# Spreading the preparation of a second layer's operands: sums of x one or two to a slot, earlier fetches, splits one to a position

## The chip, the cores and the metric

One core of one Trainium2 chip runs the whole program. The metric is the time of one execution on the device in microseconds. All times below are either whole executions, or come from one execution that the hardware profiler recorded.

## The reference, cut to what matters

A linear attention feeds two dense layers ("MoE" by name, with one expert), each a product, an activation and a product. The tokens number 2304, the model width is 512, the inner width 2048, everything is float32 (the weights come as 64-bit floats).

```python
x = attention(q, k, v)                 # 2304 x 512
h = x @ w_in1                          # 2304 x 2048
g = where(h >= 1, h, where(h <= -1, 0, (h + 1)**2 / 4))
x = g @ w_out1                         # 2304 x 512
h = x @ w_in2
g = h * tanh(log1p(exp(h)))            # Mish
out = g @ w_out2
```

## The kernel before, in words

**Precision.** A float32 operand is split into a high part (ScalarE writes a copy rounded to the fast matmul type, `high_part`, line 642) and a low part (what is left of it, a subtraction, `low_part`, line 645). Each product is then three matmuls: high by high, high by low, low by high (`three`, line 510). So each operand costs ScalarE (ACT) one pass and VectorE (DVE) or GpSimd (POOL) another before TensorE (PE) may read it.

**The first layer** goes over 6 blocks of 384 tokens (`n`) and over 16 chunks of the inner width (`c`). One step is a *slot*: `slot(i)` (line 969) does `gemm1` of chunk i (12 matmuls), its activation, and `gemm2` of the chunk three slots earlier (12 matmuls). The activation of slot i is on ACT and DVE in slot i; in slot i+1 ACT writes the high part of the result and POOL its low part (tile `ghl`, line 548). Slots 80 to 95 are the last block. What else has to be done in a slot stands in the table `ahead2`, by slot number, and is issued between `gemm1` and the activation.

**The second layer** multiplies 2 x 2 blocks of matrices with seven products in place of eight. The order of the seven is `ORDER = (1, 6, 7, 5, 4, 3, 2)`. The tokens form 3 groups (`g`) of two blocks, the inner width 8 units (`u`). `unit(g, u)` does seven products of 6 matmuls; the place of one in the row of all 168 is a *position*, 56 to a group, 7 to a unit. After each, DVE adds the PSUM result into the tiles `u`, `high`, `low`; after the last two ACT applies Mish to `high` and `low`, POOL forms four sums of them (`s`), and SyncE (SP) stores all to the DRAM buffer `gd`. What else is to be done stands in the table `places`, by position. Then `product` (line 790) multiplies by the last weights: 21 products of 72 matmuls, each in four parts (`pairs`); for these SP loads pieces from `gd` (tile `gq`, `g_load`, line 763), and ACT and DVE split them (tile `gc`, `g_split`, line 769).

**Operands of the second layer.** Four of the seven x operands of a group are differences and sums of blocks of x: `x_load` reads four blocks (tile `xq`), `x_sums` (line 686) forms them on POOL in four additions that depend on each other, `x_store` writes them to the DRAM buffer `xk`. Later `x_fetch` reads an operand back (tile `xf`), `x_high` and `x_low` split it (tile `xc`). The weights lie ready in the DRAM buffer `wk`; for a unit `w2_fetch` reads two pieces (384 KB and 512 KB), and `w2_high` and `w2_low` split them (tiles `w2p`, `w2q`). `w2_whole` and `x_operand` (lines 1010 and 1018) enter these steps in a table: the fetch at `at`, the high part at `at + apart`. In `ahead2` `apart` is 1 (slots), in `places` 8 or 6 (positions).

**What sets the order.** From slot 80 on all engines issue in the order in which the code is written: each engine has its own queue, and a step that waits holds up what stands behind it on that engine. All DMAs of this stretch are issued by SP's queue; eight semaphores, used in turn, mark their landing, so that a DMA is issued only when the eighth before it has landed. The tiles are taken in turn from two pools of buffers (`big`, 36, and `small`, 22), and a tile waits until the last reader of its buffer is done.

Of the kernel before, what the change touches and what calls it, by code (L numbers as in the profile page):

```python
# [64 lines left out]
def tile_attention_two_moes(  # L65
# [13 lines left out]
    nc = tc.nc  # L79
# [20 lines left out]
    table = const.tile([P, 1], F32, name="table")  # L100
# [145 lines left out]
    def add(eng, out, a, b, sub=True):  # L246
        eng.tensor_tensor(out=out, in0=a, in1=b, op=ALU.subtract if sub else ALU.add)  # L247
# [435 lines left out]
                t = xq[g, "q", r, c] = get([P, 2, TB], F32, "xq")  # L683
                nc.sync.dma_start(out=t, in_=yd[2 * g + c][:, 2 * r:2 * r + 2, :])

    def x_sums(g):
        b11, b12, b21, b22 = (xq[g, "q", r, c] for r in range(2) for c in range(2))
        add(nc.gpsimd, b11, b12, b11)
        add(nc.gpsimd, b12, b22, b12)
        add(nc.gpsimd, b22, b22, b11)  # L690
        add(nc.gpsimd, b21, b21, b22)

    def x_store(g):
        for i, at in enumerate(((0, 0), (1, 1), (0, 1), (1, 0))):
# [308 lines left out]
    ahead2, places, steps = {}, {}, {}  # L1003
    last = (NB - 1) * NF
    per_unit, per_group = len(ORDER), len(ORDER) * len(units)

    def put(table, key, job, *args):
        table.setdefault(key, []).append(partial(job, *args))

    def w2_whole(table, u, at, apart):  # L1010

        put(table, at, w2_fetch, 0, u, 0, 3)
        put(table, at, w2_fetch, 0, u, 3, 4)
        for x, which in enumerate((0, 2, 3, 1)):
            put(table, at + apart + x * apart // 4, w2_high, 0, u, which)
            put(table, at + apart + (x + 2) * apart // 4 + 1, w2_low, 0, u, which, nc.vector)

    def x_operand(table, at, g, k, fetch, keep, apart):
        put(table, at, x_fetch, g, k, fetch)
        put(table, at + apart, x_high, g, k, keep)  # L1020
        put(table, at + apart + 1, x_low, g, k)

    for g in range(2):
        put(ahead2, last + 3 * g, x_load, g, small)
        put(ahead2, last + 3 * g + 1, x_sums, g)
        put(ahead2, last + 3 * g + 2, x_store, g)
    for u in range(5):
        w2_whole(ahead2, u, last + 2 + 2 * u, 1)
    for x, k_ in enumerate(ORDER):
        x_operand(ahead2, last + (5 + x if x < 6 else NF), 0, k_, small, small, 1)  # L1030
    for u in range(5, len(units)):
        w2_whole(places, u, (u - 5) * 10, 8)
    put(places, per_group + 8, x_load, 2, small)
    put(places, per_group + 13, x_sums, 2)
    put(places, per_group + 24, x_store, 2)
    for g in groups[1:]:
        for x, k_ in enumerate(ORDER):
            keep = (big if x < 3 else small) if g == 1 else big if 3 <= x < 6 else small
            at = g * per_group + (3 * x - 24 if x < 3 else 2 * x - 17)
            x_operand(places, at, g, k_, small if x in (3, 5) else big, keep, 6)  # L1040
    for u in units:
        at = groups[-1] * per_group + per_unit + u * 11 // 2
# [9 lines left out]
    end = len(groups) * per_group  # L1052
    for i in pairs:
        put(places, end - 16 + i, g_load, 0, i)
        put(places, end - 8 + i, g_load, 1, i)
        put(places, (end - 8 + 2 * i if i < 3 else end - 2) if i < 4 else end - 1, g_split, 0, i)

    with region(None):
        startup()
    at = NF  # L1060
    for engines, upto in REGIONS:
# [3 lines left out]
        at = upto  # L1065
    with region(None):
        slot(len(slots) + LAG)
        for g in groups:
            for u in units:
                at = (g * len(units) + u) * per_unit  # L1070
# [40 lines left out]
```

## Time and profile before

| | |
|---|---|
| median of 3 runs | 857.52 us (855.68 to 858.70) |
| the profiled execution | 856.81 us, its span 855.0 us |
| PE busy | 839.7 us (98%) |
| PE weight loads busy | 800.3 us (94%) |
| DVE busy | 574.9 us (67%) |
| ACT busy | 487.1 us (57%) |
| POOL busy | 347.1 us (41%) |
| bytes moved | 171.24 MB, mean 200 GB/s |
| mean granted clock of TensorE | 0.998 |

The span runs from the first to the last instruction; the execution is 1.8 us longer. "Busy" is the time in which an engine had an instruction running. Of PE the matmuls overlap one another, so it counts as busy as long as one follows the other. In the rows below L601 is line 601 of the kernel, `<-` in an instruction separates what is written from what is read, and `[1.01 <-DVE xc L646]` says that the engine was idle for 1.01 us before the instruction, and that the named instruction of DVE ended that.

### The profile page before, as it was taken

The numbers are of one execution on the slowest core, as the hardware profiler recorded it, in microseconds if no ns is written. First come the engines' busy times: TensorE is split into PE (matmuls) and PEld (weight loads), VectorE is DVE, ScalarE is ACT, GpSimd is POOL, SyncE is SP. The second block draws the span as 40 slices with busy tenths as digits, with TensorE's granted clock in tenths as the row PEclk, the third lists the DMA queues.
The fourth block names the chain that finished last, engine by engine and source line by source line (L and its number), as shares of the span: only waits on it lengthen the run. The fifth ranks groups of instructions, "written<-read, shape, count | busy, mean of one in ns | idle before, by whom it ended". The sixth has DMA issues, their size and how long they took to land. (4 is left out here: it accounts for less than half of the span.)

```text
span 855.0 us, 14686 instructions
## 1 busy us (share of the span) xinstructions
PE 839.7 (98%) x5218; PEld 800.3 (94%) x5218; DVE 574.9 (67%) x967; ACT 487.1 (57%) x837; POOL 347.1 (41%) x325
## 2 busy tenths in 40 slices
PE   9899999999999999999989999999999999999998
PEld 8556689999999999999989999999999999999998
DVE  7999989786667766645336357765767759565553
ACT  3888687766766767766548344432444556453621
POOL 3001345425655654533643236577656467000000
PEclk9999999999999999999999999999999999999999
DMA  9998103256758453544496068777877797957923
GB/s 253 311 315 186 38 2 95 65 117 167 202 149 238 141 178 106 182 139 159 150 333 219 19 216 272 273 263 263 301 265 255 294 364 255 291 202 212 324 86 111
DMA packets 139993, 171.24 MB, mean 200 GB/s; under 512 B 57360, under 2 KB 109584, under 8 KB 139920
## 3 DMA queue, kind: packets, MB, share of 16 engines
q1 hardware_dynamic: 139680, 170.10, 62.4%
q8 instruction: 41, 0.67, 0.3%
q14 instruction: 32, 0.26, 0.1%
q10 hardware_dynamic: 240, 0.20, 0.1%
HBM read 108.40 MB, written 61.87 MB: 199 GB/s over the span
## 5 line engine op out<-in xcount | busy, mean ns | idle before, releaser
L601 PE MATMUL acc<-ghl,parts 128*128 128x384 f32 x1008 | 192.0, 339 | 2.2 <-POOL ghl L548 2.2
L601 PEld LDWEIGHTS acc<-ghl,parts 128*128 128x128 f32 x1008 | 176.1, 188 | 3.3 <-POOL ghl L548 2.5
L802 PE MATMUL o<-w2p,gc 128*128 128x256 f32 x1296 | 153.5, 280 | 2.0 <-ACT gc L643 1.2
L802 PEld LDWEIGHTS o<-w2p,gc 128*128 128x128 f32 x1296 | 152.5, 189 | 2.6 <-ACT gc L643 1.6
L567 DVE SCALAR_TENSOR_TENSOR rg<-h,rg 128x384 f32<-128x384 f32 x96 | 53.0, 552 | 92.6 <-ACT rg L562 82.0
L643 ACT ACTIVATE gc<-gq 128x768 fp32r<-128x768 f32 x84 | 70.5, 846 | 78.0 <-DMA gq<-gd 50.6
L511 PE MATMUL h<-xh,parts 128*128 128x384 f32 x320 | 112.9, 353 | 0.2 <-DVE rg L567 0.2
L646 DVE TENSOR_TENSOR gc<-gq,gc 128x768 fp32r<-128x768 f32 x84 | 88.5, 1089 | 32.3 <-ACT gc L643 28.2
L513 PE MATMUL h<-xh,parts 128*128 128x384 f32 x320 | 108.3, 339 | 0.0
L512 PE MATMUL h<-xl,parts 128*128 128x384 f32 x320 | 108.1, 338 | 0.0
L548 POOL TENSOR_TENSOR ghl<-rg,ghl 128x384 fp32r<-128x384 f32 x63 | 69.0, 1097 | 84.2 <-ACT ghl L545 81.5
L558 ACT ACTIVATE rg<-h,half 128x384 f32<-128x384 f32 x96 | 55.5, 578 | 81.7 <-PE h L513 74.2
L512 PE MATMUL m<-xc,w2p 128*128 128x384 f32 x288 | 97.1, 337 | 1.6 <-DVE xc L646 1.6
L513 PE MATMUL m<-xc,w2p 128*128 128x384 f32 x288 | 96.6, 335 | 0.0
L511 PE MATMUL m<-xc,w2p 128*128 128x384 f32 x288 | 96.6, 335 | 0.0
L739 ACT ACTIVATE high<-high 128x768 f32<-128x768 f32 x24 | 20.3, 847 | 95.2 <-issue 48.1
L511 PEld LDWEIGHTS h<-xh,parts 128*128 128x128 f32 x320 | 60.6, 190 | 2.3 <-DVE rg L567 0.8
L512 PEld LDWEIGHTS h<-xl,parts 128*128 128x128 f32 x320 | 60.7, 190 | 1.5
L513 PEld LDWEIGHTS h<-xh,parts 128*128 128x128 f32 x320 | 60.5, 189 | 0.0
L247 POOL TENSOR_TENSOR s<-high 128x384 f32<-128x384 f32 x24 | 26.2, 1093 | 80.2 <-ACT high L739 80.2
L156 DVE SCALAR_TENSOR_TENSOR wraw<-wraw 128x512 uint32<-128x512 uint32 x64 | 56.6, 885 | 2.0
L512 PEld LDWEIGHTS m<-xc,w2p 128*128 128x128 f32 x288 | 54.0, 188 | 2.2 <-DVE xc L646 2.2
(110 smaller groups left out, 1543.8 us busy)
## 6 DMA issues: line engine op xcount, KB each, us to landing
gq<-gd SPq DMA_DIRECT2D x84, 384.0 KB, 6.4
gd<-s SPq DMA_DIRECT2D x48, 384.0 KB, 3.3
wraw<-in_moe_w_in_dram SPq DMA_DIRECT2D x32, 512.0 KB, 6.0
wraw<-in_moe_w_out_dram SPq DMA_DIRECT2D x32, 512.0 KB, 4.7
gd<-low SPq DMA_DIRECT2D x24, 384.0 KB, 3.7
wk<-ws SPq DMA_DIRECT2D x32, 256.0 KB, 4.4
w<-wk SPq DMA_DIRECT2D x16, 384.0 KB, 4.3
v_t<-in_v_dram SPq DMA_DIRECT2D x32, 144.0 KB, 5.2
```

The lines of the kernel that those rows point to most:

```text
L156: nc.vector.scalar_tensor_tensor(out=t[:, :, 0], in0=t[:, :, 1], scalar=3, in1=t[:, :, 0], op0=ALU.logical_shift_left, op1=ALU.bitwise_xor,)
L247: eng.tensor_tensor(out=out, in0=a, in1=b, op=ALU.subtract if sub else ALU.add)
L511: nc.tensor.matmul(ps, ah, bh, start=start, stop=False)
L512: nc.tensor.matmul(ps, ah, bl, start=False, stop=False)
L513: nc.tensor.matmul(ps, al, bh, start=False, stop=stop)
L548: eng.tensor_tensor(out=gl[s], in0=temps.pop(s), in1=f(gh[s]), op=ALU.subtract)
L558: nc.scalar.activation(out=t[:, 0, :], in_=hs[s][:, :TB], func=AF.Relu, scale=0.5, bias=half)
L567: nc.vector.scalar_tensor_tensor(out=g, in0=hs[s][:, :TB], scalar=1.0, in1=r, op0=ALU.max, op1=ALU.min)
L601: nc.tensor.matmul(acc[key][x][:, :TB], *pairs[at], start=first and at == 0, stop=last and at == 2)
L643: nc.scalar.activation(out=hi, in_=x, func=AF.Copy)
L646: eng.tensor_tensor(out=lo, in0=x, in1=f(hi), op=ALU.subtract)
L802: nc.tensor.matmul(ps[j][:, :QUARTER], a[:, c, js], b, start=i == c == which == 0 and b is wh, stop=i == pairs[-1] and c == which == 1,)
```

## The change

- In the last block of the first layer (slots 80 to 95) the four additions of a group of x no longer stand in one slot: two stand in one slot, two in the next. The store follows a slot later, and the second group's load, additions and store begin one slot later than before (load in slot 84, store in slot 87).
- There the fetches of weights and of x operands are entered one slot earlier, two slots ahead of the high parts, which stay where they were.
- In the second layer the four additions of the third group stand at positions 12, 14, 16 and 18 of the second group in place of all at 13.
- The last four x operands of the second and third group (k = 5, 4, 3, 2) are fetched and split one position earlier.
- At the end of the second layer's first part the four splits for the first output product stand one to a position at the last eight positions' first four (-8, -7, -6, -5) in place of every second one (-8, -6, -4, -2).

```diff
-    def x_sums(g):
+    def x_sum(g, i):
         b11, b12, b21, b22 = (xq[g, "q", r, c] for r in range(2) for c in range(2))
-        add(nc.gpsimd, b11, b12, b11)
-        add(nc.gpsimd, b12, b22, b12)
-        add(nc.gpsimd, b22, b22, b11)
-        add(nc.gpsimd, b21, b21, b22)
+        add(nc.gpsimd, *((b11, b12, b11), (b12, b22, b12), (b22, b22, b11), (b21, b21, b22))[i])
...
     def w2_whole(table, u, at, apart):
-        put(table, at, w2_fetch, 0, u, 0, 3)
-        put(table, at, w2_fetch, 0, u, 3, 4)
+        early_ = at - (apart == 1)
+        put(table, early_, w2_fetch, 0, u, 0, 3)
+        put(table, early_, w2_fetch, 0, u, 3, 4)
...
     def x_operand(table, at, g, k, fetch, keep, apart):
-        put(table, at, x_fetch, g, k, fetch)
+        put(table, at - (apart == 1), x_fetch, g, k, fetch)
...
     for g in range(2):
-        put(ahead2, last + 3 * g, x_load, g, small)
-        put(ahead2, last + 3 * g + 1, x_sums, g)
-        put(ahead2, last + 3 * g + 2, x_store, g)
+        put(ahead2, last + 4 * g, x_load, g, small)
+        for i in range(4):
+            put(ahead2, last + 4 * g + 1 + i // 2, x_sum, g, i)
+        put(ahead2, last + 4 * g + 3, x_store, g)
...
-    put(places, per_group + 13, x_sums, 2)
+    for i in range(4):
+        put(places, per_group + 12 + 2 * i, x_sum, 2, i)
...
-            at = g * per_group + (3 * x - 24 if x < 3 else 2 * x - 17)
+            at = g * per_group + (3 * x - 24 if x < 3 else 2 * x - 18)
...
-        put(places, (end - 8 + 2 * i if i < 3 else end - 2) if i < 4 else end - 1, g_split, 0, i)
+        put(places, end - 8 + i, g_split, 0, i)
```

How the order moves, at three places. POOL's queue in the last block of the first layer, from the additions of the first group (`xq`) on; `ghl` is the low part of one slot's activation, `ws<-wq` a sum of weights:

```order
-L247 TENSOR_TENSOR ws<-wq,ws 128x256
-L548 TENSOR_TENSOR ghl<-rg,ghl 128x384 x2
-L247 TENSOR_TENSOR xq<-xq 128x768 x4
-L548 TENSOR_TENSOR ghl<-rg,ghl 128x384 x12
+L247 TENSOR_TENSOR xq<-xq 128x768 x2
+L548 TENSOR_TENSOR ghl<-rg,ghl 128x384
+L247 TENSOR_TENSOR ws<-wq,ws 128x256
+L247 TENSOR_TENSOR xq<-xq 128x768 x2
+L548 TENSOR_TENSOR ghl<-rg,ghl 128x384 x3
+L247 TENSOR_TENSOR xq<-xq 128x768 x2
+L548 TENSOR_TENSOR ghl<-rg,ghl 128x384
+L247 TENSOR_TENSOR xq<-xq 128x768 x2
```

The four additions of the second group had two low parts before them and the next one only behind all four; now three low parts stand ahead, and one between the two pairs.

SP's queue in the same block, from the store of the first group's sums (`xk_114`) on; the `w` tiles are weights of the first units (a 384 KB and a 512 KB piece each), `yd_93` is the fifth block's result:

```order
-L695 DMA xk_114<-xq 128x768 x4
-L652 DMA w_4421<-wk_0_98 128x768
-L652 DMA w_4423<-wk_0_98 128x1024
+L652 DMA w_4382<-wk_0_98 128x768
+L652 DMA w_4384<-wk_0_98 128x1024
 L230 DMA wk_7_113<-wq 128x256
 L230 DMA wk_7_113<-ws 128x512 x2
 L230 DMA wk_7_113<-wq 128x512
+L692 DMA xk_114<-xq 128x768 x4
+L652 DMA w_4477<-wk_1_99 128x768
+L652 DMA w_4479<-wk_1_99 128x1024
+L984 DMA yd_93<-y 128x384 x4
```

The first unit's weights now stand ahead of that store in place of behind it, and the second unit's ahead of the fifth block's result.

DVE's queue around the last unit, before (`u_7001` and `u_7018` are the tiles `u` of the last unit, `m_...` its products):

```order
L646 TENSOR_TENSOR gc<-gq,gc 128x768
L247 TENSOR_TENSOR u_7001<-m_6990,m_6994 128x384
L646 TENSOR_TENSOR gc<-gq,gc 128x768
L247 TENSOR_TENSOR u_7018<-u_7001,m_7011 128x384
L247 TENSOR_TENSOR high<-u_7018,m_7025 128x384
L247 TENSOR_TENSOR high<-u_7001,m_7025 128x384
L646 TENSOR_TENSOR w2p<-w_6935,w2p 128x512
L646 TENSOR_TENSOR gc<-gq,gc 128x768
L247 TENSOR_TENSOR low<-u_7018,m_7039 128x384
L646 TENSOR_TENSOR w2q<-w_6935,w2q 128x256
L247 TENSOR_TENSOR high<-high,m_7048 128x384
L646 TENSOR_TENSOR gc<-gq,gc 128x768
```

and in the change:

```order
L646 TENSOR_TENSOR gc<-gq,gc 128x768 x2
L247 TENSOR_TENSOR u_7005<-m_6990,m_6998 128x384
L646 TENSOR_TENSOR gc<-gq,gc 128x768
L247 TENSOR_TENSOR u_7022<-u_7005,m_7015 128x384
L646 TENSOR_TENSOR gc<-gq,gc 128x768
L247 TENSOR_TENSOR high<-u_7022,m_7033 128x384
L247 TENSOR_TENSOR high<-u_7005,m_7033 128x384
L646 TENSOR_TENSOR w2p<-w_6935,w2p 128x512
L247 TENSOR_TENSOR low<-u_7022,m_7043 128x384
L646 TENSOR_TENSOR w2q<-w_6935,w2q 128x256
L247 TENSOR_TENSOR high<-high,m_7052 128x384
L247 TENSOR_TENSOR low<-m_6990,m_7063 128x384
```

All four splits (`gc`) now stand ahead of the first addition into `high`; the last addition into `low` follows the last one into `high` directly, where a split stood between them.

## Rows read from the trace of the kernel before

**Rows 1.** The page: busy time and share of each engine.
```profile
PE 839.7 (98%) x5218; PEld 800.3 (94%) x5218; DVE 574.9 (67%) x967; ACT 487.1 (57%) x837; POOL 347.1 (41%) x325
```
**Rows 2.** Waits of PE: line, releaser, us in total, times, longest.
```profile
PE acc L601 <- POOL ghl L548: 2.2, 1, 2.2
...
PE m L512 <- DVE xc L646: 1.6, 2, 1.0
...
PE o L802 <- ACT gc L643: 1.2, 2, 0.8
PE o L802 <- POOL w2p L646: 0.8, 1, 0.8
```
**Rows 3.** Windows (busy times of PE, PEld, DVE, ACT, POOL; clock; DMA): slots 85 to 89.
```profile
436.13:440.31 4.18, 4.18 (x25) 4.18 (x25) 3.02 (x5) 1.17 (x3) 2.65 (x2) 1.00 1.02 376
440.31:447.13 6.82, 4.61 (x25) 4.00 (x25) 0.61 (x2) 3.50 (x7) 6.65 (x5) 1.00 0.82 319
447.13:452.96 5.83, 5.83 (x25) 5.83 (x25) 2.33 (x5) 2.78 (x5) 1.03 (x1) 0.71 1.00 364
452.96:457.50 4.54, 4.36 (x25) 4.04 (x25) 1.79 (x4) 4.30 (x9) 1.02 (x1) 1.00 0.93 322
457.50:461.82 4.32, 4.32 (x24) 4.32 (x25) 4.32 (x7) 4.29 (x10) 1.44 (x1) 1.00 0.62 194
```
**Rows 4.** Windows, the same columns: 2 us behind the wait of slot 86.
```profile
448.00:450.00 2.00, 2.00 (x8) 2.00 (x7) 0.28 (x1) 0.54 (x1) 0.00 (x0) 0.50 0.98 372
```
**Rows 5.** Timeline of POOL and ACT, slots 81 to 86: start, duration, instruction.
```profile
417.43 7.76 POOL L247 TENSOR_TENSOR xq<-xq 128x768 f32<-128x768 f32 x4
...
439.52 5.67 POOL L247 TENSOR_TENSOR xq<-xq 128x768 f32<-128x768 f32 x3 [0.83 <-DMA xq<-yd]
...
442.44 0.63 ACT L643 ACTIVATE w2p<-w 128x512 fp32r<-128x512 f32 x1 [5.11 <-DMA w<-wk]
...
445.14 1.98 POOL L548 TENSOR_TENSOR ghl<-rg,ghl 128x384 fp32r<-128x384 f32 x2
```
**Rows 6.** Timeline of SP's queue in the same stretch (time is that of issue).
```profile
419.30 6.24 SPq L695 DMA_DIRECT2D xk<-xq  x4
425.58 1.42 SPq L652 DMA_DIRECT2D w<-wk  x2
...
435.50 1.57 SPq L652 DMA_DIRECT2D w<-wk  x2
438.71 6.82 SPq L695 DMA_DIRECT2D xk<-xq  x4
```
**Rows 7.** DMA issues from 420 to 456 us: count, KB, median us to landing.
```profile
w<-wk SPq DMA_DIRECT2D x4, 512.0 KB, 6.2
...
xq<-yd SPq DMA_DIRECT2D x4, 384.0 KB, 6.3
```
**Rows 8.** Timeline of ACT, DVE and PE where the second and third group begin.
```profile
555.79 0.84 ACT L643 ACTIVATE xc<-xf 128x768 fp32r<-128x768 f32 x1
...
557.73 1.73 DVE L646 TENSOR_TENSOR xc<-xf,xc 128x768 fp32r<-128x768 f32 x1
...
559.51 0.46 PE L512 MATMUL m<-xc,w2p 128*128 128x384 f32 x1 [1.01 <-DVE xc L646]
...
618.98 0.44 PE L512 MATMUL m<-xc,w2p 128*128 128x384 f32 x1 [0.54 <-DVE xc L646]
```
**Rows 9.** Timeline of DVE, SP and ACT around the end of the last unit.
```profile
668.92 1.42 DVE L646 TENSOR_TENSOR gc<-gq,gc 128x768 fp32r<-128x768 f32 x1 [0.91 <-POOL s L247]
...
676.35 1.09 DVE L646 TENSOR_TENSOR gc<-gq,gc 128x768 fp32r<-128x768 f32 x1 [1.70 <-issue]
677.36 0.54 DVE L247 TENSOR_TENSOR low<-m,m 128x384 f32<-128x384 f32 x1
...
683.30 0.32 SPq L754 DMA_DIRECT2D gd<-s  x1
...
688.20 0.84 ACT L643 ACTIVATE gc<-gq 128x768 fp32r<-128x768 f32 x1 [5.67 <-DMA gq<-gd]
```
**Rows 10.** Splits of the last part, 660 to 712 us: duration ns min/median/max.
```profile
L646 DVE TENSOR_TENSOR gc<-gq,gc x20: 945/1195/2051, 666.2 to 710.6; 128x768 fp32r<-128x768 f32 x20
```

## The prediction, made before the changed kernel ran

> **What bounds the kernel.** First the busy line of the page [rows 1]: PE works 839.7 us of a span of 855.0, 98%; the next engine, DVE, has a third of its time free. The change leaves PE's matmuls and their order alone, so it can gain only what PE waits, and what PE loses when its clock falls after a wait. So the second view is PE's waits by releaser [rows 2]. Three stretches hold the ones that the change touches: 2.2 us in the last block of the first layer (for a low part `ghl` of POOL), 1.6 us in two waits for the low part of an x operand (`xc`), and 1.2 + 0.8 us at the start of the output products. The third view is the stretch itself, window by window [rows 3], because a wait's price is larger than the wait: an undisturbed slot takes 4.18 us, slots 86 to 89 take 6.82, 5.83, 4.54 and 4.32. Against four slots of 4.2 that is 21.5 - 16.8 = 4.7 us, of which 2.2 are the wait. In slot 87 PE is busy throughout and still takes 5.83 us, at a mean granted clock of 0.71; two microseconds of it stand at 0.50, the 1.2 GHz level [rows 4], after PE had stood still in slot 86. So some 2.3 us of the 4.7 are clock, and 0.2 small waits.
>
> Why POOL was late stands in its timeline [rows 5]: the second group's additions run from 439.52 to 445.14, three in a row behind one more, each about 1.9 us (5.67 / 3; the first group's four took 7.76), and the low part that PE wants for slot 86's second product stands behind them and starts at 445.14. On SP [rows 6] the store of these sums blocks the queue from 438.71 for 6.82 us, and ACT waits 5.11 us for weights issued at 435.50, whose landing takes 6.2 us at the median and one of the x blocks 6.3 [rows 7]. All three engines are late in the same slot, so the first wait removed uncovers a second unless that goes too.
>
> **A, the last block of the first layer.** The diff does both. The additions stand two by two: a pair is 2 x 1.9 = 3.8 us of POOL and one low part 1.0 (1.98 for two [rows 5]), 4.8 in a slot of 4.2, twice, with a slot between where POOL has little; the lag of the second pair is 0.6 us. A low part is read three slots after its `gemm1`, some 1.4 us plus the first product's 2.1 into its slot, so it may be late by two slots before PE sees it. I estimate: the x loads of the second group issue from about 432 on, as the fifth block's result must be stored before; the fourth lands 6.3 us after its issue at 436, near 442; the first pair ends at about 444, the second at 448.8, and the low part behind it at 449.8, where PE wants it at about 452.2. That leaves 2.4 us. POOL's wait of 2.2 us then goes, and with it the fall of the clock.
>
> The weights are thinner. The fetch for a unit stands a slot earlier; SP has no store of sums before it. But its second piece (512 KB) takes a buffer whose last reader is PE. For the third unit that reader is the second product of slot 85, which ends at 440.3 [rows 3]; the landing is then at 440.3 + 6.2 = 446.5. Behind it lie on ACT two splits of 0.63 [rows 5] and one slot's own passes, and a split on DVE; I make this 4.7 us together, 451.2, and they must be done before PE takes the next activation in slot 89, at 436.13 + 4 x 4.2 = 452.9. The slack is 1.7 us.
>
> Bounds of A: a full 4.7 if all four slots become undisturbed, 0 if the same stall comes back elsewhere; below zero is rival 4. I take 4.3, near the upper end, because both slacks are larger than any difference between landings in the rows, and leave 0.4 for the short waits of slots 88 and 89, which were 0.3 and 0.1.
>
> **B, the start of the second and third group.** PE waits 1.01 and 0.54 us at the third product of each, for DVE's split of an x operand that took from 557.73 to 559.46 (1.73 us); ACT's high part ran just before, at 555.79 [rows 8]. In the change the high part comes one position (1.06 us, 59.47 us between the two waits by 56 positions) earlier and DVE does the low part ahead of an addition in place of behind it. I put its start at 556.3 and its end at 558.0; PE would arrive at 559.51 - 1.01 = 558.5. Half a microsecond stays free. Bounds 0 to 1.55; I take 1.4, near the top since the step moved is a whole position and the wait a position at most.
>
> **D, the start of the output products.** Before, DVE splits a `gc` at 676.35 for 1.09 us, after 1.70 us idle, and then does the last addition into `low` at 677.36 [rows 9]. On this hang Mish, four sums on POOL, the store to `gd` at 683.30, the load of `gq` and ACT's split at 688.20, which waited 5.67 us for that load. In the change the addition into `low` follows the one into `high`, so this chain moves forward by about 1.7 us: the store to 681.6, the split to 686.5. PE's two waits for these splits (1.2 together, the longer 0.8, [rows 2]) are both smaller, so both go. The third wait, 0.8 for a weight on POOL, is later on: PE now arrives 1.2 us sooner, POOL 1.7, so 0.5 of it goes and 0.3 stays. D is 1.2 + 0.5 = 1.7, bounds 0 and 2.0.
>
> The row with the lengths of these splits says what could eat this: 945 ns at the least, 1195 at the median, 2051 at the most [rows 10], and the one at 668.92, right after a POOL sum of the unit before, took 1.42 [rows 9]. Three of the four splits move to where POOL forms sums: 3 x (1.42 - 0.95) = 1.4 us of DVE at that place. I cost it at nothing, since DVE was idle 1.70 there. The Trainium skill, "GPSIMD Engine Reference", section "1. Specifications", says that GpSimd shares its SBUF interfaces with VectorE, and that DVE instructions with two inputs in SBUF contend with it. By that rule the lengths would be no scatter but the price of the place, and D would be 0.3 in place of 1.7.
>
> **Edits at nothing.** The third group's additions at positions 12 to 18 only move work of POOL under PE's products (no wait of PE for POOL stands in that group); if that cover were gone they would cost up to their own 4 x 1.9 us. The first fetches, earlier still, lie under slots with full PE.
>
> **The sum.** 4.3 + 1.4 + 1.7 = 7.4 us. The profiled execution took 856.81, so 849.4; the median of the runs, 857.52, stands 0.7 higher, which gives 850.1, said as 850.0. A measurement of this kernel can tell about 0.3%, 2.6 us, from no change: faster means below 854.9.
>
> **Rivals.**
> 1. *The third unit's weights are late by more than the slack.* If the second piece lands over 7.9 us after 440.3 (6.2 + 1.7), PE waits in slot 89. For it: DMA is nearly full there (0.82 to 1.02 of its engines in four of the five windows, [rows 3]). Against it: the median of 6.2 comes from the same load. A wait half as long as today's, with half its clock, gives back 2.3: 852.3.
> 2. *The moved splits pay POOL's price*, as worked out in D: 1.4 us back, 851.4. For it the 1.42 of [rows 9], against it the idle 1.70.
> 3. *The change doesn't do what it says*: the low part was only the first of three late things [rows 5, 6], ACT's weights stop PE in the same stretch with the same clock, and D's chain is held by the POOL weight. A and D give nothing, B its 1.4: 856.1. For it the 5.11 us wait of ACT; against it that the fetch stands a slot earlier.
> 4. *Slower.* The three fetches from the third unit on each wait for a buffer that PE frees, with SP held behind each (its queue then also holds the stores and loads behind). If each costs a stop like today's, wait and clock, 3 x 4.7 = 14.1 us come on top of 850.0: 864.1. It decides when the stops come to more than 7.4 in all. For it: SP stood still for 6.24 and 6.82 us behind one waiting store [rows 6]. Against: PE frees a buffer every 4.2 us and never waited for weights here [rows 2].
>
> **Chances.** The forecast 0.66, rival 1 0.13, rival 2 0.08, rival 3 0.08, rival 4 0.05. The upper bounds (4.7 + 1.6 + 2.0 = 8.3) give 849.2; the runs before lie 1.2 to 1.8 around their median, so the range begins at 847.8. Upward it takes in rivals 1 and 2 with as much room, 853.5, and leaves out rivals 3 and 4. Faster is the forecast with rivals 1 and 2, 0.87; same is rival 3, 0.08; slower is rival 4, 0.05.
>
> **What the next profile would show.** A right: no wait of PE for `ghl`, slots 86 to 89 at 4.2 us, the clock at 1.00 from 440 to 460, `xq` in pairs on POOL, ACT's wait for weights below a microsecond. B right: no wait of PE for `xc`. D right: `low` directly behind `high` on DVE, the store to `gd` 1.7 us sooner in relation to the first output product, and a wait for `w2p` of 0.3 or none. Wrong: a wait of PE for `h` or `rg` between slots 88 and 91 with the clock below 1, or SP's queue standing on a weight fetch with loads behind it.

## The result and the profile after

The changed kernel takes 849.01 us (median of 3 runs, 848.21 to 850.33) against 857.52: a ratio of 0.9903, 95% interval 0.9888 to 0.9919, 8.5 us faster. The forecast was 850.0, with a range from 847.8 to 853.5.

The page's busy line of the changed kernel, then all waits of PE in it (line, releaser, us in total, times, longest), answer to [rows 1] and [rows 2]:

```profile
PE 834.9 (99%) x5218; PEld 796.9 (94%) x5218; DVE 582.9 (69%) x967; ACT 485.9 (57%) x837; POOL 350.6 (41%) x325
```
```profile
PE qT L467 <- POOL q_e L455: 3.0, 2, 1.7
PE h L529 <- DVE rg L567: 2.6, 3, 1.5
PE warm L946 <- POOL ident masks.py:199: 1.4, 1, 1.4
PE o L799 <- POOL w2p L646: 0.6, 1, 0.6
PE mT L324 <- DVE km L319: 0.4, 1, 0.4
PE mb L340 <- DVE mx L332: 0.2, 1, 0.2
```

The waits for `ghl`, `xc` and `gc` are gone; of those that the prediction spoke of, 0.6 us for a weight `w2p` is left. The windows of the changed kernel for slots 85 to 89, in the columns of [rows 3]:

```profile
437.02:441.24 4.22, 4.22 (x25) 4.22 (x25) 1.62 (x4) 2.68 (x6) 0.03 (x1) 1.00 1.03 385
441.24:445.45 4.21, 4.21 (x25) 4.21 (x25) 2.66 (x2) 1.47 (x3) 4.13 (x2) 1.00 0.94 320
445.45:449.67 4.22, 4.22 (x25) 4.22 (x25) 3.30 (x3) 4.19 (x9) 4.14 (x4) 1.00 0.71 263
449.67:453.92 4.25, 4.25 (x26) 4.25 (x25) 4.25 (x4) 2.24 (x5) 4.03 (x4) 1.00 0.92 309
453.92:458.10 4.18, 4.18 (x25) 4.18 (x25) 4.18 (x7) 2.69 (x6) 1.02 (x1) 1.00 1.02 394
```

Every slot takes 4.2 us at a granted clock of 1.00, where slots 86 to 89 took 6.82, 5.83, 4.54 and 4.32. POOL's timeline there, against [rows 5], and below it the one addition of the second group that stood ahead of those three in the kernel before:

```profile
441.21 4.40 POOL L247 TENSOR_TENSOR xq<-xq 128x768 f32<-128x768 f32 x2 [6.12 <-DMA xq<-yd]
445.57 1.02 POOL L548 TENSOR_TENSOR ghl<-rg,ghl 128x384 fp32r<-128x384 f32 x1
446.54 4.11 POOL L247 TENSOR_TENSOR xq<-xq 128x768 f32<-128x768 f32 x2
450.62 2.90 POOL L548 TENSOR_TENSOR ghl<-rg,ghl 128x384 fp32r<-128x384 f32 x2
```
```profile
436.83 1.86 POOL L247 TENSOR_TENSOR xq<-xq 128x768 f32<-128x768 f32 x1 [1.67 <-DMA xq<-yd]
```

The additions start no earlier than before, and SP still stands still for their store (it starts at 443.38 and holds the queue for 7.62 us); what PE waits for no longer stands behind either.

PE's work is the same in both kernels, so subtracting the starts of the same matmul in two traces shows where time is lost. The table does that for the stretches of all kernels here, in us, with the times of the changed kernel's second trace at the head. The first 40 us are left out: PE reaches that matmul after 37.5 to 40.9 us, in no order that follows the edits, and much of the difference between single runs is that: 38.58 and 40.13 in the two traces of the changed kernel, whose executions are 1.51 us apart. "To end" means to the start of PE's last matmul; the twelve extra matmuls of `filler` aren't matched with any, but the time that they take counts.

| kernel | 437 to 463 (A) | 545 to 600 | 600 to 630 | 676 to 712 (D) | 712 to end | 40 to end |
|---|---|---|---|---|---|---|
| before | 30.42 | 56.47 | 30.93 | 38.15 | 132.77 | 813.70 |
| changed | 25.86 | 54.98 | 30.12 | 36.07 | 132.10 | 804.10 |
| changed, again | 25.86 | 54.98 | 30.12 | 36.01 | 132.09 | 804.05 |
| fetch_undone | 25.77 | 55.06 | 30.21 | 36.12 | 132.47 | 805.17 |
| sums_undone | 25.75 | 54.99 | 30.18 | 35.74 | 132.81 | 804.32 |
| filler | 30.24 | 56.37 | 30.96 | 37.53 | 132.39 | 812.73 |
| b_undone | 25.86 | 56.50 | 30.75 | 36.44 | 133.61 | 808.21 |
| d_undone | 25.86 | 54.98 | 30.12 | 37.46 | 131.88 | 805.44 |
| third_at_13 | 25.86 | 54.98 | 30.12 | 36.37 | 132.09 | 804.33 |
| low_on_dve | 25.86 | 54.98 | 30.12 | 35.76 | 132.10 | 803.73 |
| sums_on_dve | 25.83 | 55.01 | 30.10 | 36.62 | 132.44 | 804.83 |
| gc_all_96 | 25.86 | 54.98 | 30.12 | 36.37 | 134.78 | 807.20 |
| gc_all_32 | 25.86 | 54.98 | 30.12 | 35.94 | 128.18 | 799.63 |
| best | 25.86 | 54.98 | 30.12 | 35.80 | 128.18 | 799.61 |

From before to changed: A 4.56, B 1.49 + 0.81 = 2.30, D 2.08, the products from 712 on 0.67, together 9.6; the profiled execution of the changed kernel happened to begin 0.9 us later, which leaves 8.7; the two profiled executions (856.81 and 848.21) are 8.6 apart. Two traces of the changed kernel agree within 0.06 us in every column, which the medians of runs don't.

### The profile page after: what moved, and what is told of

It reads as the page before. It is cut to its first block, busy times and chain, and to the rows that moved or that the text cites. A ratio compares the mean times of both kernels' runs of the same rounds, so it can differ in the third digit from the quotient of the medians.

```text
span 846.4 us, 14671 instructions
## 1 busy us (share of the span) xinstructions
PE 834.9 (99%) x5218; PEld 796.9 (94%) x5218; DVE 582.9 (69%) x967; ACT 485.9 (57%) x837; POOL 350.6 (41%) x325
## 4 chain that ended last, share of the span: by engine, by line
PE 90%; DMA 3%; DVE 3%; SPq 2%; ACT 1%; issue 1%; POOL 0%; DVEq 0%; ACTq 0%; POOLq 0%
PE acc L601 21%; PE o L799 19%; PE m L512 7%; PE m L511 7%; PE m L513 7%; PE h L511 7%; PE h L513 7%; PE h L512 7%; PE h L529 3%; PE acc L590 2%; PE xps L482 2%; DMA gq<-gd 1%; PE kv L366 1%; DMA q_t<-in_q_dram 1%; PE qT L467 1%; SPq L308 1%
## 5 line engine op out<-in xcount | busy, mean ns | idle before, releaser
L646 DVE TENSOR_TENSOR gc<-gq,gc 128x768 fp32r<-128x768 f32 x84 | 90.3, 1107 | 32.1 <-ACT gc L643 30.6
L545 ACT ACTIVATE ghl<-rg 128x384 fp32r<-128x384 f32 x84 | 43.5, 518 | 19.3 <-DVE rg L567 17.6
```

Source lines behind the costliest of these rows:

```text
L545: nc.scalar.activation(out=gh[s], in_=temps[s], func=AF.Copy)
L646: eng.tensor_tensor(out=lo, in0=x, in1=f(hi), op=ALU.subtract)
```

## The experiments

**The changed kernel again** gave 848.24 us, ratio 0.9889 (0.9875 to 0.9903), 9.45 us below the kernel before in that group of runs.

> The changed kernel itself, as the yardstick of this group. Both theories: 849.0 us, 8.5 below the kernel before (between 7.5 and 9.5).

**Part A, one half at a time.** First the fetches back to one slot ahead:

```diff
-        early_ = at - (apart == 1)
+        early_ = at
...
-        put(table, at - (apart == 1), x_fetch, g, k, fetch)
+        put(table, at, x_fetch, g, k, fetch)
```

> The changed kernel, but in the first layer's last block the fetches stand one slot ahead of the high parts again; the additions stay in pairs. Theory 1 (both halves of the edit are needed): the second unit's weights are issued only near 437 and land 6.2 us later, near 443.5; ACT's passes behind them hold the activation until about 447.7, where PE wants its bank at 445.5. PE then waits some 2 us there for DVE or ACT (tile rg or h), the clock falls behind it, and 4.5 of the 8.5 us are lost: 853.5. Theory 2 (the pairs alone do it): 849.0, within 0.8, and no wait of PE in slots 85 to 90.

849.97 us, ratio 0.9913 (0.9899 to 0.9926). Column A is as short as with the change and PE waits for nothing there: theory 2. ACT does wait again for weights, and POOL does the low parts in good time:

```profile
440.86 0.63 ACT L643 ACTIVATE w2p<-w 128x512 fp32r<-128x512 f32 x1 [3.10 <-DMA w<-wk]
```
```profile
445.07 4.12 POOL L247 TENSOR_TENSOR xq<-xq 128x768 f32<-128x768 f32 x2
449.15 1.47 POOL L548 TENSOR_TENSOR ghl<-rg,ghl 128x384 fp32r<-128x384 f32 x1
```

The dates in the expectation were wrong: with the additions moved, the second unit's weights were issued at 434.75, not near 437, and ACT's wait of 3.10 us ended before PE came round. The 1.1 us that this kernel loses elsewhere (0.3 of it in the 82 us between 463 and 545) stands beside no wait; its cause stays open, and with it why the median is a little above what theory 2 allowed.

Then the additions back into one slot, fetches early:

```diff
-        put(ahead2, last + 4 * g, x_load, g, small)
-        for i in range(4):
-            put(ahead2, last + 4 * g + 1 + i // 2, x_sum, g, i)
-        put(ahead2, last + 4 * g + 3, x_store, g)
+        put(ahead2, last + 3 * g, x_load, g, small)
+        for i in range(4):
+            put(ahead2, last + 3 * g + 1, x_sum, g, i)
+        put(ahead2, last + 3 * g + 2, x_store, g)
```

> The changed kernel, but the additions of a group of x stand in one slot again and the second group's load, additions and store a slot earlier, as before; the fetches stay early. Theory 1 (POOL's queue is the cause): the wait for the low part ghl is back with 2.2 us and the clock's share of 2.3: 853.5. Theory 2 (the transfers are the cause, the additions were late only because their loads stood behind fetches and a store on SP): the additions end sooner, PE waits less than 0.5: 849.0 to 849.8.

849.90 us, ratio 0.9909 (0.9895 to 0.9923); column A is again as short: theory 2 here too, though only just. Its POOL timeline, then the first of the low parts there by itself and the matmul that waited for it in the kernel before:

```profile
434.68 1.85 POOL L247 TENSOR_TENSOR xq<-xq 128x768 f32<-128x768 f32 x1 [2.05 <-DMA xq<-yd]
437.10 6.24 POOL L247 TENSOR_TENSOR xq<-xq 128x768 f32<-128x768 f32 x3 [0.57 <-DMA xq<-yd]
443.30 4.31 POOL L548 TENSOR_TENSOR ghl<-rg,ghl 128x384 fp32r<-128x384 f32 x3
```
```profile
443.30 1.46 POOL L548 TENSOR_TENSOR ghl<-rg,ghl 128x384 fp32r<-128x384 f32 x1
444.85 0.41 PE L601 MATMUL acc<-ghl,parts 128*128 128x384 f32 x1
```

The last three additions, one block of POOL as before, begin at 437.10 where they began at 439.52 [rows 5]; this execution was 1.08 us later at PE's 40 us mark, so the additions are 3.5 us earlier in relation to PE, and the low part 2.9. That is enough to cover the step of 2.5 us that PE lost there, but barely: the low part ends at 444.76, and the matmul starts at 444.85, without idle time before it. In the changed kernel the same low part is POOL's of 433.64, done at 435.09 for a matmul at 444.76. Whether the other three executions here (849.21 to 850.74) were covered as well, no trace shows. The blocks of x landed earlier: the first unit's weights, issued at 425.58 right ahead of their loads in the kernel before [rows 6], went out at 407.62, and the loads took 5.0 us at the median in place of 6.3. So the stall needed both: late blocks, and a low part that stands behind all additions. Either half of the edit takes it away whole in these traces, the early fetches alone with 0.1 us to spare, the pairs with more; they don't add up.

**The stall filled with work.** The kernel before, with twelve more matmuls (0.17 us apart, 2.1 in all) in slot 86:

```diff
+        for _ in range(4 if s == slots[86] else 0):
+            three(
+                hs[s][:, :TB], parts[c, 0][:, 0, :P], parts[c, 0][:, 1, :P],
+                xh[ph, n][0][:, 0, :], xl[ph, n][0][:, 0, :], True, True,
+            )
```

> The kernel before with 12 more matmuls (2.1 us) on PE at the start of slot 86, into the bank that the slot's first product then overwrites: PE works where it stood idle. Theory 1 (half of the loss is the clock that falls after the wait): the low part comes when it came, PE doesn't stand still, the granted clock stays at 1.00 in slot 87, and the kernel gains about 2 us over before: 855.5. Theory 2 (slot 87 is long for another reason, or the clock falls anyway): 857.5, or up to 2 us more.

856.59 us, ratio 0.9989 (0.9978 to 1.0000): theory 1 is right on the clock and wrong on the time. Windows from slot 86 on, and PE's timeline after the second:

```profile
445.20:449.20 4.00, 3.92 (x23) 3.59 (x22) 0.38 (x1) 3.05 (x7) 3.92 (x4) 1.00 0.74 291
449.20:454.80 5.60, 4.89 (x28) 4.57 (x27) 2.37 (x5) 2.77 (x5) 1.65 (x2) 1.00 0.99 353
454.80:460.10 5.30, 4.49 (x25) 4.17 (x25) 2.42 (x5) 4.33 (x8) 1.01 (x1) 1.00 0.97 383
```
```profile
454.82 0.44 PE L511 MATMUL h<-xh,parts 128*128 128x384 f32 x1 [0.74 <-DVE rg L572]
```

The clock stays at 1.00 where it stood at 0.50 [rows 4], and the stretch A is still 30.24 us. In place of the wait for `ghl` PE now waits twice for DVE's activation (1.5 us counted, in slots 88 and 89), behind ACT's late weights: the second lateness of which the prediction spoke, which had been hidden behind the first one and its slow clock. These pauses, 0.74 and 0.79 us, left the clock alone. They take back what the clock gained: column A is 4.4 us longer than with the change, 2.1 of it the extra matmuls, most of the rest the two pauses.

**Part B undone** (`2 * x - 18` back to `2 * x - 17`):

> The changed kernel, but the last four x operands of the second and third group are fetched and split one position later, as before. Theory 1: the two waits for xc come back with 1.0 and 0.5 us: 850.5 to 850.9. Theory 2 (the waits were there because of what was late before them, and are gone with it): 849.0.

853.18 us, ratio 0.9944 (0.9932 to 0.9957). The two waits are back where they were:

```profile
PE m L512 <- DVE xc L646: 1.4, 2, 1.1
```

Their two columns are 1.52 and 0.63 longer than with the change, theory 1. The kernel loses 2.0 us more after 676, of which its wait for `w2p` (0.8 us where the changed kernel has 0.5 or 0.6) is the smaller part; its median stands 4.2 and 4.9 above the two of the changed kernel and outside both theories' times. The section on the hardware comes back to that.

**Part D undone** (the splits back at every second position):

> The changed kernel, but the first output product's splits stand at every second one of the last positions again. Theory 1: the last addition into low waits behind a split, the chain over Mish, POOL's sums, the store to gd and the load of gq is 1.7 us later, PE waits 0.8 and 0.4 for gc and some more for w2p: 850.7 to 851.1. Theory 2 (the weights on POOL set the start of the output products): 849.0 to 849.3, PE's time moves from gc to w2p.

849.58 us, ratio 0.9903 (0.9889 to 0.9917). Its waits of PE in the output products:

```profile
PE o L799 <- ACT gc L643: 0.8, 1, 0.8
PE o L799 <- POOL w2p L646: 0.7, 1, 0.7
```

One of the two waits for `gc` is back with 0.8 us, the wait for `w2p` hardly moves. Column D grows by 1.45, theory 1 with 1.45 of the 1.7 to 2.1 us that it named; the medians, 0.6 to 1.3 apart, can't show that much.

**The third group's additions together** (all four at position 13):

> The changed kernel, but the four additions of the third group stand at position 13 together again. Theory 1 (POOL's work lies under PE's there): 849.0, within 0.5, no wait of PE for POOL between 555 and 650. Theory 2 (they hold up the four sums of a unit on POOL and with them buffers): slower by 0.5 to 2 us, with a wait of PE for s, xc or w2p in that stretch.

849.72 us, ratio 0.9906 (0.9891 to 0.9921). Columns up to 630 are the same to 0.01 us and PE waits for POOL nowhere there: the edit is worth nothing in its own stretch, as costed. Column D is 0.3 us longer, with a wait for `w2p` of 0.7, and the median is 0.7 above the 849.0 that theory 1 gave within 0.5; from 40 us on the trace shows 0.3.

**One low part on DVE** (`nc.vector if x == 5 else nc.gpsimd` in the last `w2_low`):

> The changed kernel, but one of the sixteen low parts of weights in the output products (the sixth) is DVE's and not POOL's. Theory 1 (the wait of 0.6 us for w2p that is left comes from POOL's queue, which does 1.9 us for each): the wait goes, 848.4. Theory 2 (the weights or ACT's high parts are late, or DVE has no room beside its splits): 849.0 or up to 1 us more, with a wait of PE for w2p or gc in its place.

848.96 us, ratio 0.9899 (0.9887 to 0.9912). Neither theory as it stands: the wait doesn't go, it gets shorter and stands on the other engine.

```profile
PE o L799 <- DVE w2p L646: 0.3, 1, 0.3
```

Column D is 0.25 to 0.31 us shorter; a median can't show that.

**The second group's additions on DVE** (`nc.vector if g == 1 else nc.gpsimd` in `x_sum`):

> The changed kernel, but the four additions of the second group of x are DVE's and not POOL's. In the changed kernel DVE's low parts of weights beside these additions took 2.10 us (512 wide) and 2.07 (256 wide), where the same forms took 0.68 and 0.42 elsewhere. Theory 1 (two engines that read and write SBUF there hold each other up): without POOL's additions beside them they take 0.7 and 0.4 in slots 86 to 88, though the DMA traffic is the same; PE waits for nothing there, so the time is the changed kernel's within 1 us. Theory 2 (the DMA traffic, at its highest there, slows them): they stay at 2 us, and DVE, with the additions as well, makes PE wait for rg or h at slots 88 to 90, with 1 to 4 us lost.

One run, 851.21 us, above the 1 us that theory 1 allowed; it reached PE's 40 us mark 2.3 us later than the changed kernel's first trace, and from there on it is 0.7 to 0.8 us longer, 0.6 of it in column D with a wait for `w2p` of 1.1. DVE's low parts of weights in slots 86 to 88, first in the changed kernel, then here:

```profile
446.84 2.10 DVE L646 TENSOR_TENSOR w2p<-w,w2p 128x512 fp32r<-128x512 f32 x1
448.86 2.07 DVE L646 TENSOR_TENSOR w2q<-w,w2q 128x256 fp32r<-128x256 f32 x1
```
```profile
445.19 0.69 DVE L646 TENSOR_TENSOR w2p<-w,w2p 128x512 fp32r<-128x512 f32 x1
445.79 0.42 DVE L646 TENSOR_TENSOR w2q<-w,w2q 128x256 fp32r<-128x256 f32 x1
```

2.10 against 0.69 and 2.07 against 0.42: theory 1 on the splits. The transfers don't explain it: the DMA engines were busy for 0.69 of the time from 446.84 to 450.90 in the changed kernel and for 0.79 from 445.19 to 446.20 here. The splits were slow because of POOL. The additions themselves take 0.96 us on DVE where it isn't disturbed. PE's stretch A is the same.

**Where the tiles `gc` lie** (the section on the hardware says why): the same order of work, and only the first byte of each of these tiles shifted by 64 where needed.

```diff
+    def aligned(name):
+        t = small([P, 2 * TB + 16], F32R, name)
+        first = 16 * ((0x4fb023ec247ec247e841fa283f9283f2a0fc941f5a >> turn[0]) % 2 == 1)
+        turn[0] += 1
+        return t[:, first:first + 2 * TB].rearrange("p (c t) -> p c t", c=2)
...
-            gc[at, i] = hi, lo = [small([P, 2, TB], F32R, "gc") for _ in range(2)]
+            gc[at, i] = hi, lo = [aligned("gc") for _ in range(2)]
```

(The number holds for each tile in turn whether its buffer begins at 96 above a multiple of 128; with `== 0` in place of `== 1` all lie at 96.)

> The changed kernel with one thing else: the tiles gc of the output products (the operand that PE loads as weights) all begin at a byte address that is 32 above a multiple of 128; in the changed kernel 798 of the 1512 matmuls read theirs there and 714 at 96 above one. The order of all work stays. In the changed kernel's trace one of these matmuls follows the last by 115.0 ns where the address is of the first kind and by 119.1 where it is of the second. Theory 1 (PE's pace there hangs on that address): 714 x 4.1 ns = 2.9 us faster than the changed kernel (848.2 to 849.0 so far): 845.3 to 846.1. Theory 2 (the address only goes along with something else, such as what the other engines do at that time): no difference, within 0.7.

843.59 us, ratio 0.9825 (0.9807 to 0.9842).

> The same with all tiles gc at 96 above a multiple of 128. Theory 1: 798 x 4.1 ns = 3.3 us slower than the changed kernel, 851.5 to 852.3, and 6 us above the kernel with all at 32. Theory 2: as the changed kernel, 848.2 to 849.0, within 0.7.

850.70 us, ratio 0.9910 (0.9894 to 0.9926). Theory 1 in both: from 40 us to the end 4.5 us less than the changed kernel with all at 32 and 3.1 more with all at 96, 7.6 apart where 6.2 were expected (both medians lie below the times that theory 1 gave, by 1.7 and 0.8 us). One group of the products' matmuls, those that read `w2q`, count and duration in ns (least/median/most), in the changed kernel, with all at 32 and with all at 96:

```profile
L799 PE MATMUL o<-w2q,gc x144: 274/277/290, 725.1 to 792.4; 128*128 128x256 f32 x144
```
```profile
L807 PE MATMUL o<-w2q,gc x144: 276/276/276, 723.0 to 788.2; 128*128 128x256 f32 x144
```
```profile
L807 PE MATMUL o<-w2q,gc x144: 274/283/290, 726.3 to 794.8; 128*128 128x256 f32 x144
```

**Both together**, the shifted tiles and the low part on DVE:

> The changed kernel with all gc at 32 above a multiple of 128 and the sixth low part of weights on DVE. Theory 1: both gains add up, 2.9 + 0.5: 844.8 to 845.6. Theory 2 (with PE faster by 3% in the output products, POOL's low parts, DVE's splits or the loads become the bound there): new waits of PE for w2p or gc take a part of it back, 846 to 847.

843.13 us, ratio 0.9829 (0.9811 to 0.9847): no better than the shift alone (799.61 against 799.63 from 40 us on). PE, now faster, waits 1.0 us for that one weight, whether POOL or DVE prepares it. The fastest kernel is the changed one with the shift, some 5 us below it and nearly 15 below the kernel before.

## Why the prediction was right, point by point

**The bound.** The prediction said that PE's waits and the clock behind one were all that the change could gain. Of the 9.6 us from PE's 40 us mark on, 8.9 lie in the three stretches named. The other 0.67 lies behind the last wait, in the pace of the output products, for which the prediction had no term. By the last section some 0.3 of it is the place of the weight operands in memory: 798 of the 1512 matmuls have theirs at the faster kind of address, 720 in the kernel before. That is luck of the placing; the rest is open.

**The sum: 7.4 taken, 8.9 measured in the same three terms.** All three were too small, by 0.26, 0.90 and 0.38. That 850.0 lies only 1.0 from 849.01 is in part luck: the medians of the first group put 8.5 us between the kernels, those of the next 9.45, and the traces 9.6.

**A: 4.3 taken, 4.56 measured.** Right in size, less so in the split between wait and clock, where two misses cancel: the step at the wait is 2.5 us (2.37 at the matmul that waits, 0.10 at the next), not 2.2; the slow matmuls behind it, 0.32 us apart in place of 0.17 until 450.5, cost 1.8, not 2.3; the short wait before slot 89 costs 0.4. Of the reasons one half was too strong. That the weights had to come earlier as well isn't so for this kernel; pairs alone remove the stall, and early fetches alone do, with 0.1 us to spare.

The slacks were smaller than worked out. The second pair ended at 450.65, not 448.8, since SP issued the x loads from 433.38, behind two weight pieces, and a pair took 4.1 to 4.4 us in place of 3.8. The low part behind it was done at 452.07, and by the prediction's own rule (2.1 + 1.4 us into the slot that begins at 449.67) due at 453.2: 1.1 us left, not 2.4. The weights of the third unit were on ACT at 446.17, as forecast (446.5), and yet the activation that PE needs at 453.92 came from DVE at 453.10: 0.8 us left where 1.7 were forecast. DVE, not ACT, was late, because its splits ran beside POOL's additions:

```profile
452.55 0.55 DVE L567 SCALAR_TENSOR_TENSOR rg<-h,rg 128x384 f32<-128x384 f32 x1
```

One sign that the prediction named for A didn't show: ACT's wait for weights was to stay below a microsecond, and the one for the fourth unit's is 1.27 (5.11 before). PE waits for nothing behind it.

```profile
456.77 0.63 ACT L643 ACTIVATE w2p<-w 128x512 fp32r<-128x512 f32 x1 [1.27 <-DMA w<-wk]
```

**B: 1.4 taken, 2.30 measured**, above the upper bound of 1.55. The mechanism holds (both waits gone; back, in b_undone, with the one position). The term was mis-sized: it took the waits as counted. In the kernel before, the step at the wait of [1.01] is 1.30 us and at [0.54] it is 0.80, read from the starts in both traces. The idle time is counted from the end of the matmul before, which overlaps the next by some 0.16 us (0.33 us long, 0.17 apart), and the first matmul after the wait takes 0.46 us [rows 8] in place of 0.33. A pause of PE costs nearly 0.3 us more here than its row says.

**D: 1.7 taken, 2.08 measured**, a little above its upper bound of 2.0, for the same reason: the two steps are 1.10 and 0.66 us for waits of 1.2 counted, and 0.33 comes from the third wait. The store to `gd` starts at 675.52 and ACT's split at 680.60; PE's lead over the trace of before was 5.9 us there, so they are 1.9 and 1.7 us sooner, as worked out. The third wait keeps 0.6 us, not 0.3; that part of D was taken too large.

**Costed at nothing**, and so in their own stretch: the third group's additions.

**The rivals.** Rival 1 didn't happen: ACT split the third unit's weights from 446.17 on without a wait for them. Rival 3 fell with the windows of slots 86 to 89. Rival 4: SP stood still for 7.62 us and no fetch was late for it. Rival 2's price was real and its effect wasn't. The moved splits were slow beside POOL's sums, two of them 3.04 us in place of 1.9 (0.95 each, [rows 10]) and the third 1.30, 1.5 us in all where rival 2 had 1.4, but DVE had the time, and D came whole:

```profile
660.26 3.04 DVE L646 TENSOR_TENSOR gc<-gq,gc 128x768 fp32r<-128x768 f32 x2 [1.31 <-ACT gc L643]
```

The rule of the Trainium skill, "GPSIMD Engine Reference", section "1. Specifications", that DVE instructions with two inputs in SBUF contend with GpSimd, is borne out by the experiment with the additions on DVE (2.10 us to 0.69, 2.07 to 0.42).

## What to carry to other kernels

When two engines are late for the same slot, the one named as releaser isn't the whole cause: here moving either engine's work ahead removed the stall (one of them by 0.1 us), and filling the wait with work only uncovered the second one. Price a pause of a bound PE from the starts of its instructions, not from the idle time alone, and compare variants by stretches of the trace when their medians differ by less than the start of a run does. Before the last microseconds are sought in the order of the work, look at how evenly identical matmuls follow each other.

## What the runs showed of the hardware that wasn't expected

**The pace of the product's matmuls hangs on where the weight operand lies.** In the output products PE loads the tiles `gc` as weights and streams the prepared `w2p` and `w2q` past them. A variant that changes no work of the output products still changed their time: 712 to the end reads 131.88 to 133.61 in the table, the same for every trace with the same placing of buffers. The tiles `gc` lie in buffers 3136 bytes apart, so they begin 32 or 96 bytes above a multiple of 128. In the changed kernel's traces a matmul of 256 columns follows the last after 115.0 ns on average in the first case and 119.1 in the second (from the starts of one and the next); with all tiles at 32 the median is 113, with all at 96 it is 120. On average it is 113.7 against 119.2, which over 1512 matmuls is 8.4 us; PE's wait for `w2p`, 1.0 us with all at 32 and 0.2 with all at 96, takes 0.8 of it back, and 7.6 are left, nearly as much as the whole change. That it is the address is shown by the two kernels that differ in nothing else; whether PE's reading of the tile or the writing of it by ACT and DVE makes the difference was not separated. Nor is the address of a matmul's own tile all of it: matmuls at 32 follow each other after 113.7 ns where all tiles lie there, after 115.0 in the changed kernel, 115.8 in the kernel before and 116.7 in b_undone. In the second layer's first part, with 384 columns, where the weight operand always lies at 96, the same comparison for the moved operand (173.7 and 174.4 ns) shows little. No run tells what other distances, 0 or 64, would do.

Open is a rest: b_undone has only 72 more matmuls at 96 than the changed kernel, 0.3 us by these numbers, and loses 2.0 after 676, 0.2 to 0.3 of it in the longer wait for `w2p`. Its matmuls at 32 take up to 117.5 ns on average in the last third. What makes them slow there wasn't tried.

**The clock.** A pause of PE with 2.2 us counted was followed by a granted clock of 0.50 and cost 1.8 us more behind it [rows 3, 4]; with the pause filled with matmuls (filler) the clock stayed at 1.00; pauses of 1.01 us (in the kernel before), 0.8 and 0.7 us (in filler) left it at 1.00. The window of the kernel before behind the first of these, in the columns of [rows 3]:

```profile
559.50:562.50 3.00, 2.99 (x17) 2.99 (x18) 2.28 (x5) 1.10 (x2) 0.17 (x1) 1.00 0.99 319
```
